# Fused attention and two MLP stages on one core: scales of v spread by ones-products instead of through DRAM, weights of norm loaded contiguously, first maxima of v taken later

## The chip, the cores and the metric

One core of one Trainium2 chip runs the whole program. The metric is the device time of one execution in microseconds (us), lower is better; the runs of a kernel are summed up by their median.

## What is computed

```python
# q, k, v: 4 batches x 12 heads x 448 x 64; x: 4 x 448 x 768
s = einsum('bhij,hg->bgij', 0.125 * q @ k.T, w_pre)          # heads mixed before softmax
p = softmax(s)
a = einsum('bhij,hg->bgij', p, w_post) @ v                   # heads mixed after it
x = a as (batch, 448, 768)
u, v = split(gelu_tanh(x @ w_in)); v_n = norm(v) * g_ln      # 768 -> 2 x 512
x = x + (u * (w_sg @ v_n + b_sg)) @ w_out
t = x @ w_theta; y = w_tok_r @ (x * cos t) + w_tok_i @ (x * sin t)
u = x + y; out = u + max(u @ w_ch, 0)
```

## The kernel before, in words

The program is one long list of instructions that Python writes out in order; every engine takes its own in that order. `attention` walks over 180 **blocks**: a block is 10 rows of the score matrix with all 12 heads (120 partitions x 448). A **tile** is up to 120 rows (12 blocks, or 9 for the rest), four tiles make a batch. The loop over `s` writes for each step several stages of different blocks, so that they overlap:

- `relayout(s+7)`: SP issues the DMA `blk<-s` (L217), which puts rows of the scores into the block's layout; five buffers.
- `premix(s+4)`: two products `psB` (L223) on TensorE; `rowmax(s+4)` `nmx` (L229) on DVE.
- `expo(s+3)` `e` (L236) on ACT; then `recip` on POOL (L244), `recip2` on DVE (L250), `p_hi` on POOL (L255), `p_lo` `pl` on DVE (L262).
- `postmix(s)`: twelve products `psC` (L277 to L280); `at_hi` (L302, ACT) and `at_lo` `al` (L308, DVE) for block s-1.
- `scores`: products `psA` of the tile after next (L203), copied out by ACT (L207, L209).

Between them three tables are called at fixed steps: `early` (mostly DMA issues, written behind `relayout`), `work` (products, behind `p_lo`) and `late` (at the end of the step). `put(table, s, fn)` enters a call. `attn_v` multiplies with v (L329), `turn_x` transposes the result into the PSUM tile `psT` (L342), which ACT empties (L349, L352).

v goes into the products as two fp16 halves, scaled by a power of two for each of its 768 channels. `load_vT` (L133) brings v transposed, channels on partitions, two pieces of 128 channels at a time; there are two buffers, so the third load of a batch waits for the first `v_max` (L148, DVE), which takes the maxima. `v_scale` (L87 to L95, L156) makes the scales `sv`, 128 partitions x 6. `v_mul` (L178, POOL) needs them along the free axis of every partition, as `vbc`, 128 x 768. So `v_scale_out` (L162) writes `sv` to DRAM with an access pattern of 4-byte elements, and `v_scale_in` (L166) reads the 3 KB back into all partitions. SP issues both; the second waits until the first has landed.

`put_v(b, s, m, gap)` enters this: `v_scale` at s, out at s+2, in at s+5, and from step m on `load_v`, `v_mul`, `v_hi`, `v_lo` piece by piece. For batch 0 the loads of vT stand at steps -7 to -5, the maxima at -6 to -4, s is -3 and m is 5; the loop starts at step -7. For batches 1 to 3 s is 7 steps ahead of the batch's first block and m 2 to 4 steps behind it.

Ahead of the loop stand the warm-up products (L421), the loads of q and k, the scores of the first tile, and `consts`. Decoding jobs of the later stages' float64 weights are woven in (`da`, `dp`, `dl`, `dh`; L588 to L631).

After attention the dense stages run as a list of units with calls ahead (`pre`) and behind (`post`) each. Where the first MLP starts, `rest` (L710, L712) loads `gln` (512 weights of norm, 128 x 4, each a 4-byte element in DRAM) and `bsg`; right behind them SP issues `wsgraw` (L727, L730), which ACT casts and DVE splits (`wsg`, L557, L560) for the `gate` products. `gln` is used in L834.

Of the kernel before, what the change touches and what calls it, by code (L numbers as in the profile page):

```python
# [6 lines left out]
F32 = mybir.dt.float32  # L7
F32R = mybir.dt.float32r
# [3 lines left out]
AF = mybir.ActivationFunctionType  # L12
# [4 lines left out]
B, H, S, D = 4, 12, 448, 64  # L17
NP = H // 2
DM = H * D
IB = 10  # L20
TI = IB * 12
TILES = [(t0, min(TI, S - t0)) for t0 in range(0, S, TI)]
LDS = (7, 4, 3, 2, 1, 4, 4, 5)
LD, LB, LE, LH, LL, EB, PB, SB = LDS
# [9 lines left out]
VM = 5  # L34
# [3 lines left out]
def attention(tc, nc, io, xT, B, extra, tail):  # L38
# [17 lines left out]
    with ExitStack() as es:  # L56
# [14 lines left out]
        cp = pool("a_const", 1)  # L71
# [8 lines left out]
        vsc_p = pool("a_vsc", 2)  # L80
        psB = pool("psB", 2, space=PSUM)
        psC = pool("psC", 2, space=PSUM)
        psD = pool("psD", 1, space=PSUM)
# [15 lines left out]
        wh = cp.tile([TI, H, IB], F16, name="wh")  # L99
        wl = cp.tile([TI, H, IB], F16, name="wl")  # L100
        dwp = cp.tile([128, NP], F32, name="dwp")
        ident = cp.tile([TI, TI], F32, name="ident")

        def consts():
            kpost = sm_p.tile([TI, H, IB], F32, tag="kpost", name="kpost", bufs=1)
            nc.sync.dma_start(out=kpost, in_=io["kpost"].rearrange("p (g i) -> p g i", g=H))
            nc.sync.dma_start(out=ident, in_=io["ident"][:TI, :TI])
            wrep = sm_p.tile([128, H, H], F32, tag="wrep", name="wrep", bufs=1)
            nc.sync.dma_start(out=wrep, in_=io["w_postT"].rearrange("g h -> (g h)").partition_broadcast(128)
                                .rearrange("p (g h) -> p g h", g=H))  # L110
            mx = sm_p.tile([128, H], F32, tag="wmx", name="wmx", bufs=1)
            nc.vector.tensor_reduce(out=mx, in_=wrep, axis=AX.X, op=ALU.max, apply_absolute_value=True)
            sw = sm_p.tile([128, H], F32, tag="sw", name="sw", bufs=1)
            dw = sm_p.tile([128, H], F32, tag="dw", name="dw", bufs=1)
            pow2(sw, dw, mx, H)
            nc.vector.tensor_tensor(out=kpost, in0=kpost,
                                    in1=sw[:TI].unsqueeze(2).to_broadcast([TI, H, IB]), op=ALU.mult)
            nc.vector.tensor_copy(wh, kpost)
            nc.vector.tensor_tensor(out=wl, in0=kpost, in1=wh, op=ALU.subtract)
            for e in range(2):  # L120
                nc.vector.tensor_scalar(out=dwp[64 * e:64 * e + 64], in0=dw[64 * e:64 * e + 64, e::2],
                                        scalar1=8.0, scalar2=None, op0=ALU.mult)


        raws, kt, qt = {}, {}, {}
# [12 lines left out]
            nc.sync.dma_start(out=qt[b, t][:, :NP * n], in_=io["qT"][b, :, NP * t0:NP * (t0 + n)])  # L138

        vt, dsc, vsb = {}, {}, {}  # L140
        vs_dram = es.enter_context(tc.tile_pool(name="a_vsd", bufs=1, space=bass.MemoryType.DRAM))
        vs_d = vs_dram.tile([B, DM], F32, name="vs_d")

        def v_max(b, c):
            if c == 0:
# [11 lines left out]
            dsc[b] = ds  # L157
            raws["sv", b] = sv

        def v_scale_out(b):  # L160
            with nc.allow_non_contiguous_dma(reason="768 scales"):
                nc.sync.dma_start(out=vs_d[b].rearrange("(c p) -> p c", p=128), in_=raws.pop(("sv", b)))  # L162

        def v_scale_in(b):
            bc = vsc_p.tile([128, DM], F32, tag="vbc", name="vbc", bufs=1)
            nc.sync.dma_start(out=bc, in_=vs_d[b].partition_broadcast(128))  # L166
            vsb[b] = bc

        def load_v(b, c):
            vt[b, c] = [v_p.tile([128, 4, 128], F16, tag=f"{t}{c}", name=t) for t in ("vh", "vl")]  # L170
# [190 lines left out]
        early, work, late = {}, {}, {}  # L361

        def put(d, s, fn, *a):
            d.setdefault(s, []).append((fn, a))
# [9 lines left out]

        def put_v(b, s, m, gap):
            put(late, s, v_scale, b)
            put(early, s + 2, v_scale_out, b)
            put(early, s + 5, v_scale_in, b)
            for c in range(NP):
                put(early, m - 2, load_v, b, c)  # L380
                put(late, m, v_mul, b, c)
                put(late, m + 2, v_hi, b, c)
                put(late, m + 3, v_lo, b, c)
                m += gap

        for T in range(2, nt):
            b, t = tiles[T]
# [3 lines left out]
            if t == 0:  # L391
                for c in range(NP):
                    put(early, unit(T - 1, c), load_k, b, c)
                for c in range(0, NP, 2):
                    s = unit(T - 1, c)
# [3 lines left out]
        for T in range(nt):  # L399
            b, t = tiles[T]  # L400
            l = last[tiles[T]]
            for c in range(NP):
                s = l + DD[t][c]
# [27 lines left out]
            scores(0, 0, c)  # L431
        consts()
        for c in range(0, NP, 2):
            put(early, -LD + c // 2, load_vT, 0, c)
            put(late, -LD + 1 + c // 2, v_max, 0, c)
        put_v(0, -LD + 4, VM, 2)
        for s in range(-LD, NB + 12):
            if s == -LD:
                for fn, a in early.get(s - 1, []):
# [36 lines left out]
KD, KF = DM // 128, HF // 128  # L476
# [187 lines left out]
def moe1(d, left, right):  # L664
# [37 lines left out]
    def rest():  # L702
        tail_ps.close()
        for name, bufs in (("w", 1), ("u", 1), ("vn", 1), ("t", 2), ("dec", 1)):
            d.open(name, bufs, left)
        d.open_psum(8, right)
        w = d.pools["w"]
        gln = w.tile([128, KF], F32, name="gln")
        with nc.allow_non_contiguous_dma(reason="512 values"):
            nc.sync.dma_start(out=gln, in_=io["g_ln"].rearrange("(k p) -> p k", p=128))  # L710
        bsg = w.tile([128, S], F32, name="bsg")
        nc.sync.dma_start(out=bsg, in_=io["b_sg"].partition_broadcast(128))  # L712
        small.update(gln=gln, bsg=bsg)
# [182 lines left out]
    for b in range(B):  # L896
# [8 lines left out]
        if b + 1 < B:  # L905
            i = u0[b] + KF
# [291 lines left out]
def layout(i):  # L1198
# [9 lines left out]
    for x in range(IB):  # L1208
# [11 lines left out]
        "kpost": kpost.reshape(TI, TI),  # L1220
        "w_postT": f(i["w_post"].T),
        "w_in": w64(i["moe_w_in"]),
        "g_ln": f(i["moe_g_ln"]),
        "w_sgT": f(i["moe_w_sg"].T),
        "b_sg": f(i["moe_b_sg"]),
        "w_out": w64(i["moe_w_out"]),
# [23 lines left out]
```

## Time and profile before

| what | value |
|---|---|
| median of 3 runs | 1045.97 us (1043.34 to 1046.72) |
| the profiled execution's own time | 1047.47 us |
| its span, first to last instruction | 1045.6 us |
| mean granted TensorE clock | 0.978 of full speed |
| PE / DVE / POOL / ACT busy, share of the span | 94% / 74% / 60% / 56% |

PE is TensorE's products, PEld its weight loads, SPq the issue of a DMA by SyncE. A busy share is an average over stages with different limits; what a stage is bound by is read from its own stretch. The attention blocks run from about 15 to 500 us, the first MLP to about 745 us, the rest is the second.

### The profile page before, as it was taken

The page shows a single profiled execution, that of the slowest core. Times are in us where ns is not written, and L with a number is a line of the kernel's source. Part 1 is how long each engine was busy: PE and PEld are TensorE (multiplying, and loading weights), DVE is VectorE, ACT ScalarE, POOL GpSimd, SP SyncE. Part 2 cuts the span into 40 slices and gives each one's busy share as a digit, 9 for nine tenths or more (in the row PEclk, how much of TensorE's full clock was granted, in tenths as well). Part 3 has the DMA queues.
Part 4 walks back from the last instruction along what each step waited for, and adds up shares of the span by engine and source line. Part 5 has one row for each costly group of instructions (what it writes and reads, how often), then busy time and mean ns, then how long its engine had stood idle before and what let it go on. Part 6 is the DMA issues. An engine that isn't in the chain of part 4 may idle for free.

```text
span 1045.6 us, 21830 instructions
## 1 busy us (share of the span) xinstructions
PE 982.3 (94%) x7848; PEld 742.7 (71%) x7848; DVE 775.5 (74%) x1458; ACT 586.6 (56%) x1374; POOL 622.4 (60%) x818
## 2 busy tenths in 40 slices
PE   7789999999999999997978999799999999999998
PEld 2445655565656555566756979587888999999997
DVE  2799878987888878985989998898896724925611
ACT  4577778786777778775754645454364412613310
POOL 0596558754686548854656877775666643753622
PEclk9899999999999999998989999999999999999999
DMA  5757565556556564347353676758956131130021
GB/s 191 154 167 221 142 139 183 180 168 129 161 193 203 131 158 152 131 108 265 113 155 89 213 225 199 229 188 274 335 184 226 41 106 31 32 106 16 31 76 53
DMA packets 135504, 159.47 MB, mean 153 GB/s; under 512 B 30309, under 2 KB 120933, under 8 KB 135397
## 3 DMA queue, kind: packets, MB, share of 16 engines
q1 hardware_dynamic: 135397, 158.08, 50.3%
q8 instruction: 63, 1.03, 0.4%
q14 instruction: 44, 0.36, 0.1%
HBM read 86.66 MB, written 32.85 MB: 114 GB/s over the span
## 4 chain that ended last, share of the span: by engine, by line
PE 57%; DVE 20%; DMA 9%; POOL 5%; issue 4%; ACT 3%; SPq 1%; DVEq 0%; ACTq 0%; POOLq 0%
PE ps L564 27%; PE psB L223 10%; PE psA L203 5%; PE psD L329 5%; DVE da L604 3%; PE psC L280 3%; PE psC L277 3%; DMA blk<-s 2%; PE psC L278 2%; DVE pl L262 2%; DVE da L602 2%; DVE dp L610 2%; DMA xres<-xT 2%; DVE dp L618 2%; DMA xraw<-xT 1%
## 5 line engine op out<-in xcount | busy, mean ns | idle before, releaser
L255 POOL TENSOR_SCALAR ph<-e,rc 120x448 f16<-120x448 f32 x180 | 163.9, 911 | 147.3 <-DVE rc L250 99.8
L223 PE MATMUL psB<-blk,kpre 120*120 120x448 f32 x360 | 177.3, 575 | 13.0 <-DMA blk<-s 8.2
L229 DVE TENSOR_REDUCE nmx<-psB 120x1 f32<-120x448 f32 x180 | 111.3, 618 | 49.9 <-PE psB L223 40.8
L262 DVE SCALAR_TENSOR_TENSOR pl<-e,rc,ph 120x448 f16<-120x448 f32 x180 | 147.4, 819 | 0.0
L236 ACT ACTIVATE e<-psB,nmx 120x448 f32<-120x448 f32 x180 | 114.3, 635 | 43.1 <-DVE nmx L229 43.0
L308 DVE SCALAR_TENSOR_TENSOR al<-psC,ah 128x480 f16<-128x480 f32 x180 | 116.1, 645 | 8.2 <-ACT ah L302 7.9
L277 PE MATMUL psC<-wh,ph 120*128 120x120 f16 x720 | 97.7, 218 | 10.9 <-DVE al L308 7.1
L302 ACT ACTIVATE ah<-psC 128x480 f16<-128x480 f32 x180 | 103.0, 572 | 7.6 <-PE psC L280 4.9
L209 ACT ACTIVATE s<-psA 120x896 f32<-120x896 f32 (+1 forms) x90 | 82.5, 917 | 42.5 <-PE psA L203 41.1
L564 PE MATMUL ps<-wtok,z 128*128 128x448 f32 x504 | 104.8, 368 | 0.4 <-POOL z L560 0.4
L564 PEld LDWEIGHTS ps<-wtok,z 128*128 128x128 f32 x504 | 94.4, 188 | 10.1 <-POOL z L560 0.8
L277 PEld LDWEIGHTS <-ph 120*128 120x128 f16 x720 | 68.8, 99 | 44.3 <-issue 18.6
L278 PE MATMUL psC<-wl,ph 120*128 120x120 f16 x720 | 97.1, 218 | 2.4 <-issue 2.4
L329 PEld LDWEIGHTS <-ah 128*128 128x128 f16 x1536 | 76.6, 99 | 31.2 <-issue 31.2
L203 PE MATMUL psA<-k,q 64*120 64x448 f32 (+1 forms) x384 | 96.2, 580 | 1.0 <-ACT s L209 1.0
L564 PE MATMUL ps<-wth,x2s 128*128 128x384 f32 x504 | 92.5, 338 | 2.0 <-POOL x2s L560 2.0
L564 PE MATMUL ps<-u,wch 128*128 128x448 f32 x432 | 89.9, 368 | 0.0
L564 PEld LDWEIGHTS ps<-wth,x2s 128*128 128x128 f32 x504 | 87.2, 188 | 2.8 <-POOL x2s L560 2.6
L560 POOL TENSOR_TENSOR z<-zz,z 128x384 fp32r<-128x384 f32 x56 | 61.9, 1125 | 45.8 <-ACT z L557 45.8
L564 PEld LDWEIGHTS ps<-u,wch 128*128 128x128 f32 x432 | 81.0, 188 | 8.1
L278 PEld LDWEIGHTS <-ph 120*128 120x128 f16 x720 | 71.2, 99 | 14.4 <-issue 14.2
L329 PE MATMUL psD<-vl,ah 128*128 128x64 f16 x768 | 78.0, 194 | 1.1 <-POOL vl L185 1.1
(124 smaller groups left out, 2171.9 us busy)
## 6 DMA issues: line engine op xcount, KB each, us to landing
blk<-s SPq DMA_DIRECT2D x176, 210.0 KB
draw<-in_w_in SPq DMA_DIRECT2D x24, 256.0 KB
vraw<-in_vN SPq DMA_DIRECT2D x24, 256.0 KB
k<-in_kvT SPq DMA_DIRECT2D x24, 224.0 KB
vT<-in_kvT SPq DMA_DIRECT2D x12, 448.0 KB
xraw<-xT SPq DMA_DIRECT2D x24, 224.0 KB
xres<-xT SPq DMA_DIRECT2D x24, 224.0 KB
x2T<-xres SPq DMA_DIRECT2D x24, 224.0 KB
```

The source lines that it names most:

```text
L203: nc.tensor.matmul(ps[e][:n, :S], q[p, o:o + n], k[p], start=True, stop=True)
L223: nc.tensor.matmul(ps[:r, :S], kpre[:r, :r], sblk.pop(s)[:r], start=True, stop=True)
L229: nc.vector.tensor_reduce(out=m[:r], in_=mix[s][:r, :S], axis=AX.X, op=ALU.max, negate=True)
L236: nc.scalar.activation(out=e[:r], in_=mix.pop(s)[:r, :S], func=AF.Exp, bias=nmx.pop(s)[:r], accum_out=sm[:r])
L255: nc.gpsimd.tensor_scalar(out=p[:r], in0=ex[s][0][:r], scalar1=rec[s][:r], scalar2=0.0, op0=ALU.mult, op1=ALU.add)
L262: nc.vector.scalar_tensor_tensor(out=p[:r], in0=ex.pop(s)[0][:r], scalar=rec.pop(s)[:r], in1=ph[s][:r], op0=ALU.mult, op1=ALU.subtract)
L277: nc.tensor.matmul(ps[:, jc, :, :n], cols(a, jc), wh[:r, :, :n], start=(jc == 0), stop=False)
L278: nc.tensor.matmul(ps[:, jc, :, :n], cols(a, jc), wl[:r, :, :n], start=False, stop=False)
L302: nc.scalar.activation(out=at_view(s, at[b, t][0]), in_=src, func=AF.Copy, scale=2.0 ** -17)
L308: nc.vector.scalar_tensor_tensor(out=al, in0=src, scalar=2.0 ** -17, in1=ah, op0=ALU.mult, op1=ALU.subtract)
L329: nc.tensor.matmul(ps[:, o:o + 64], a[:, i0:i0 + 128], v[:, jc, 64 * e:64 * e + 64], start=(o == 0 and m == 0), stop=(o == 320 and m == le ...
L564: self.nc.tensor.matmul(ps, l, r, start=(i == 0), stop=(i == len(terms) - 1))
```

## The change

The scales no longer go through DRAM. `v_diag` lets ACT write, for each of the six pieces, the identity times the piece's scales (a diagonal 128 x 128 matrix); `v_spread` multiplies a matrix of ones with three such diagonals at once (128 x 384), which puts each scale into all partitions of the PSUM tile `psT`, and ACT copies that to `vbc`. The identity grows from 120 x 120 to 128 x 128, and one more ACT operation makes the ones. In batches 1 to 3 (g = 1) the parts are spread over steps s+1 to s+6, in batch 0 over s+1 to s+3. `gln` comes as 128 contiguous runs of 16 bytes, its array being transposed on the host. For batch 0 the loads of vT move to steps -5 to -3, the maxima to -2 to 0, and `v_scale` from -3 to 1; m stays.

```diff
-        ident = cp.tile([TI, TI], F32, name="ident")
+        ident = cp.tile([128, 128], F32, name="ident")
+        ones = cp.tile([128, 128], F32R, name="ones")
...
-            nc.sync.dma_start(out=ident, in_=io["ident"][:TI, :TI])
+            nc.sync.dma_start(out=ident, in_=io["ident"])
+            nc.scalar.activation(out=ones, in_=ident, func=AF.Copy, scale=0.0, bias=1.0)
...
-        def v_scale_out(b):
-            with nc.allow_non_contiguous_dma(reason="768 scales"):
-                nc.sync.dma_start(out=vs_d[b].rearrange("(c p) -> p c", p=128), in_=raws.pop(("sv", b)))
-
-        def v_scale_in(b):
-            bc = vsc_p.tile([128, DM], F32, tag="vbc", name="vbc", bufs=1)
-            nc.sync.dma_start(out=bc, in_=vs_d[b].partition_broadcast(128))
-            vsb[b] = bc
+        def v_diag(b, c):
+            if c == 0:
+                raws["dg", b] = vsc_p.tile([128, NP, 128], F32R, tag="dg", name="dg", bufs=1)
+                vsb[b] = vsc_p.tile([128, DM], F32, tag="vbc", name="vbc", bufs=1)
+            nc.scalar.activation(out=raws["dg", b][:, c], in_=ident, func=AF.Copy, scale=raws["sv", b][:, c:c + 1])
+
+        def v_spread(b, half):
+
+            ps = psD.tile([128, 512], F32, tag="psT", name="psV", bufs=1)
+            nc.tensor.matmul(ps[:, :384], ones, raws["dg", b][:, 3 * half:3 * half + 3], start=True, stop=True)
+            nc.scalar.activation(out=vsb[b][:, 384 * half:384 * half + 384], in_=ps[:, :384], func=AF.Copy)
...
             put(late, s, v_scale, b)
-            put(early, s + 2, v_scale_out, b)
-            put(early, s + 5, v_scale_in, b)
+            g = 1 if b else 0
+            for c in range(NP):
+                put(late, s + 1 + g * (c // 2), v_diag, b, c)
+            for half in range(2):
+                put(work, s + 2 + half + g * (2 + half), v_spread, b, half)
...
-            put(early, -LD + c // 2, load_vT, 0, c)
-            put(late, -LD + 1 + c // 2, v_max, 0, c)
-        put_v(0, -LD + 4, VM, 2)
+            put(early, -LD + 2 + c // 2, load_vT, 0, c)
+            put(late, -2 + c // 2, v_max, 0, c)
+        put_v(0, 1, VM, 2)
...
-        with nc.allow_non_contiguous_dma(reason="512 values"):
-            nc.sync.dma_start(out=gln, in_=io["g_ln"].rearrange("(k p) -> p k", p=128))
+        nc.sync.dma_start(out=gln, in_=io["g_ln"])
...
-        "g_ln": f(i["moe_g_ln"]),
+        "g_ln": f(i["moe_g_ln"].reshape(KF, 128).T),
```

## Rows read from the trace of the kernel before

**Rows 1.** The page: busy time, share of the span and instructions of two engines.
```profile
PE   982.3 (94%) x7848; PEld 742.7 (71%) x7848; DVE 775.5 (74%) x1458; ACT 586.6 (56%) x1374; POOL 622.4 (60%) x818
```

**Rows 2.** The chain that ended last, 20 to 40 us: start, length, what.
```profile
20.91 3.46 DMA vT<-in_kvT
...
27.23 11.20 DMA blk<-s
```

**Rows 3.** SP's timeline, 14 to 37 us: start, length, line, what, how many.
```profile
14.58 0.94 SPq L217 DMA_DIRECT2D blk<-s  x1
...
26.74 0.38 SPq L162 DMA_DIRECT2D vs_d<-sv  x1
27.23 1.69 SPq L217 DMA_DIRECT2D blk<-s  x2
...
36.90 0.35 SPq L166 DMA_DIRECT2D vbc<-vs_d  x1
```

**Rows 4.** Stretches: PE, PEld, DVE, ACT, POOL busy, clock, DMA share, GB/s.
```profile
30.00:32.00 2.00, 2.00 (x16) 1.02 (x15) 1.79 (x5) 1.55 (x4) 1.54 (x5) 1.00 0.63 8
...
34.00:36.00 2.00, 0.00 (x0) 0.00 (x0) 0.49 (x1) 0.58 (x3) 1.11 (x2) 1.00 0.41 13
...
38.00:40.00 2.00, 1.43 (x2) 0.63 (x3) 0.00 (x0) 0.00 (x0) 0.00 (x0) 0.50 0.96 226
```

**Rows 5.** Timelines of PE and DVE: first premix; maxima of blocks 0 and 7.
```profile
17.88 0.98 PE L223 MATMUL psB<-blk,kpre 120*120 120x448 f32 x2 [1.10 <-DMA blk<-s]
...
22.94 0.61 DVE L229 TENSOR_REDUCE nmx<-psB 120x1 f32<-120x448 f32 x1
...
40.42 0.62 DVE L229 TENSOR_REDUCE nmx<-psB 120x1 f32<-120x448 f32 x1 [5.93 <-PE psB L223]
```

**Rows 6.** Groups by line, 18 to 41 us: DVE's operations, busy and mean ns.
```profile
L229 DVE TENSOR_REDUCE nmx<-psB 120x1 f32<-120x448 f32 x8 | 5.0, 620 | 6.2 <-PE psB L223 6.2
...
L148 DVE TENSOR_REDUCE vmx<-vT 128x2 f32<-128x896 f32 x3 | 3.3, 1087 | 9.1 <-DMA vT<-in_kvT 9.1
...
L262 DVE SCALAR_TENSOR_TENSOR pl<-e,rc,ph 120x448 f16<-120x448 f32 x4 | 2.7, 678 | 0.0
...
L308 DVE SCALAR_TENSOR_TENSOR al<-psC,ah 128x480 f16<-128x480 f32 x3 | 1.9, 650 | 0.0
...
L250 DVE RECIPROCAL rc<-rc 120x1 f32<-120x1 f32 x5 | 0.8, 158 | 0.3 <-POOL rc L244 0.2
```

**Rows 7.** Stretches behind the writes of batches 1, 2 and 3 (columns as in 4).
```profile
140.00:145.00 5.00, 4.04 (x47) 2.20 (x46) 2.83 (x6) 2.78 (x7) 2.23 (x4) 1.00 0.76 164
250.00:260.00 10.00, 7.82 (x72) 3.93 (x70) 5.03 (x13) 5.43 (x15) 3.36 (x6) 1.00 0.58 84
370.00:375.00 5.00, 3.02 (x27) 1.59 (x24) 1.43 (x4) 2.22 (x7) 0.95 (x2) 1.00 0.51 95
```

**Rows 8.** SP's timeline where the first MLP starts: loads behind gln.
```profile
520.29 0.43 SPq L710 DMA_DIRECT2D gln<-in_g_ln  x1
...
521.37 1.33 SPq L727 DMA_DIRECT2D wsgraw<-in_w_sgT  x3
```

**Rows 9.** Timelines of ACT and DVE there: the first cast and split of wsgraw.
```profile
527.79 0.58 ACT L557 ACTIVATE wsg<-wsgraw 128x448 fp32r<-128x448 f32 x1 [5.40 <-DMA wsgraw<-in_w_sgT]
...
528.40 0.62 DVE L560 TENSOR_TENSOR wsg<-wsgraw,wsg 128x448 fp32r<-128x448 f32 x1 [4.03 <-ACT wsg L557]
```

**Rows 10.** The stretch from that split to a wait for decoded wout (columns as in 4).
```profile
528.50:570.00 41.50, 32.19 (x122) 23.86 (x120) 40.70 (x62) 23.29 (x57) 29.41 (x29) 0.88 0.33 101
```

**Rows 11.** Timelines of ACT and PE: what the added work resembles.
```profile
150.78 0.86 ACT L349 ACTIVATE x<-psT,dsc 128x120 f32<-128x120 f32 x3
...
758.93 6.52 PE L564 MATMUL ps<-wth,x2s 128*128 128x384 f32 x36
```

**Rows 12.** Who waited for whom, whole span: TensorE's weight loads on ACT.
```profile
PEld psB L223 <- ACT e L236: 8.0, 7, 2.5
```

More of the change, by code (lines that the diff above doesn't have):

```diff
@@ L140, in attention @@
         vt, dsc, vsb = {}, {}, {}
-        vs_dram = es.enter_context(tc.tile_pool(name="a_vsd", bufs=1, space=bass.MemoryType.DRAM))
-        vs_d = vs_dram.tile([B, DM], F32, name="vs_d")
         def v_max(b, c):
```

## The prediction, as put on record before the run

> **What bounds the kernel now.** I read the page first: TensorE is busy for 94% of the span and no other engine for more than 74% [rows 1], so time is to be won where TensorE stands still, and each place has to be asked what it waits for. The chain of waits, read next, names a transfer in the start-up: a relayout of the scores that is issued at 27.23 us and takes 11.20 us [rows 2]. A relayout normally lands much faster: the first is issued at 14.58 and its premix starts at 17.88, after 3.3 us [rows 3, 5]. SP's timeline shows what stands ahead of the slow one: at 26.74 the 3 KB of scales go to DRAM, and SP can issue their read only at 36.90, when that write has landed, 10.2 us later [rows 3]. The stretches show the DMA engines meanwhile: busy for 0.63 and 0.41 of the time while 8 and 13 GB/s move; when the jam is over, 0.96 at 226 GB/s [rows 4]. So the engines work on many tiny pieces, and the relayouts issued behind them stand in line. TensorE does nothing from 34 to 36 us, and comes back at 0.50 of its clock, the level of 1.2 GHz [rows 4].
>
> The same write comes again ahead of batches 1, 2 and 3. There the relayouts are some blocks ahead, and most of the delay is hidden; what is left is TensorE's idle time in the stretch behind each write [rows 7]. The last place is the start of the first MLP, where gln, 512 pieces of 4 bytes, is issued just ahead of wsgraw [rows 8].
>
> **Start-up (term A).** Removed: the write, the read, and SP's wait between them. Moved: three loads of vT by two steps, past the relayouts of blocks 2 to 4 in SP's queue, and three maxima and the scales on DVE, from a time in which DVE waits to one in which it works. What limits the new start is DVE's own list up to the maximum of block 7, which now starts at 40.42 [rows 5]. The first premix ends at 17.88 + 0.98 = 18.9; today block 0's maximum starts only at 22.94, since the early maxima of v, which wait for their loads, stand ahead of it in DVE's queue [rows 5]. From 18.9 on DVE has to do, by mean durations [rows 6]: 8 maxima of blocks, 8 x 0.62 = 5.0; 4 pl, 4 x 0.68 = 2.7; 2 al, 1.3; 5 reciprocals, 0.8; 3 maxima of v, 3 x 1.09 = 3.3; the scales, six operations, which I price like the reciprocals, 1.0. That is 14.1 us, so 33.0; I add 0.5 for waits and take 33.5: a gain of 40.42 - 33.5 = 6.9.
>
> The ends of this term: at most the whole wait of 5.93 ahead of block 7's maximum and the whole 4.1 by which block 0's is late, 10.0 together [rows 5]. At the low end stands the third load of vT: with two buffers it waits for the first maximum, which now stands behind block 2's, and the relayouts of blocks 5, 6 and 7 wait behind it in SP's queue. By my list the first maximum of v is done at 22 to 23, so the load is issued then and is there at 23 + 3.5 = 26.5 [rows 2], about when DVE comes to it. If SP is held longer, DVE loses up to another such load, 3.5, and the gain is 3.4. I take nothing for the half clock after the hole: the list of DVE, not TensorE, sets the pace there. ACT writes six diagonals, each like one of the three small copies that take 0.86 together, 0.29, so 1.7 us, and empties two products, each of 384 columns like those three together, 0.86, so another 1.7 [rows 11]. Just ahead of the hole ACT is busy for 1.55 of 2 us [rows 4]; at 14.1 / 8 = 1.76 a block it has some 0.4 free in each, and each block's exponentials stand a step ahead of their use, which covers the rest; I charge 0.4. Should ACT have nothing free, it is up to 3.4. The making of the ones (one more 0.29) falls between the last copy of the first scores and the next ones, and the larger identity is a transfer that nobody waits for; both cost nothing as long as that holds, 0.3 if not. A is -6.5, between -10 and -3.
>
> **Batches 1 to 3 (term B).** Idle TensorE time behind the three writes: 5 - 4.04, 10 - 7.82 and 5 - 3.02, that is 0.96 + 2.18 + 1.98 = 5.1 us [rows 7]. Without the write these relayouts come in time and this goes. Added for TensorE: two products of 384 columns per batch; 36 of that shape take 6.52, so 0.18 each, six of them 1.1 us. TensorE is the bound there, so they are paid in full. ACT's 3.4 us per batch lie over six steps with two small operations at a time. The first product stands two steps behind the diagonals that it reads, the second three, so I see no wait; its PSUM tile is also turn_x's, which uses it one step earlier, and ACT empties it within that step. No row shows this wait; it is bounded by nothing below and above by 2.5 us for each, the longest of 7 waits of TensorE for ACT's exponentials (8.0 in all) [rows 12]. I take 0.4 in all, near the lower end because of those steps between. B is -5.1 + 1.1 + 0.4 = -3.6, between -5.1 and 0.
>
> **Weights of norm (term C).** The first wsgraw is issued at 521.37 and cast at 527.79, 6.4 us later, and DVE, which has nothing else, stands 4.03 us until it can split it [rows 8, 9]. From there to 570 DVE is busy for 40.70 of 41.50 us [rows 10] and sets when wout is decoded, for which TensorE then waits. So what DVE gets earlier the end gets earlier; the lower clock in that stretch costs nothing extra. Without the jam wsgraw should take 3.3 us as the first relayout did, and about 0.7 for bsg ahead of it: 4.0, a gain of 2.4. The new gln has 128 pieces in place of 512; no row shows 16-byte pieces, and by the scales' 768 pieces in 10.2 us [rows 3] they would cost 1.7 us at most, beside bsg's transfer in good part. C is -2.4, between -4.0 (the whole wait) and 0 (16-byte pieces hold up as much).
>
> **Sum.** -6.5 - 3.6 - 2.4 = -12.5. The profiled execution took 1047.47, 1.5 more than the median of 1045.97; against its own time the sum gives 1035.0, against the median **1033.5**, which I predict.
>
> The Trainium skill bears on the terms' common root. Its page "DMA: Bandwidth & Descriptors", section "Anatomy of one DMA — SWDGE (gpsimd) path", fits a transfer, on another queue's path, as 2.0 us plus its bytes at 436 GB/s; the 3 KB would then be there in 2.0 us, and nothing would be won by taking them away. The trace has 10.2 us for it [rows 3] and decides against that fit. The same page's section "Bandwidth" puts a small packet at some 10.5 ns, which as an estimate makes 768 of them 8.1 us beside the 2.0; by that figure the trace agrees.
>
> **The rivals.** (1) *The tiny pieces are innocent*: the late relayouts come from the loads of vT and of the jobs that stand ahead, and these remain. Then nothing is won and the six products cost 1.1: 1047. Against it speak the busy engines at 8 GB/s [rows 4], and that the wait sits behind such a write four times of four. By the skill's fit above this would be the case; the same rows weaken it. Chance 0.05.
> (2) *The third load of vT takes the write's place* in SP's queue and A is only -3: 1037. For it speaks that SP takes its list in order; against it, that the load is about ready when DVE comes. Chance 0.2.
> (3) *More comes back*: A near -10, B and C near -4 each, so -18: 1028. It needs a DVE that overlaps its operations better than my list. Chance 0.12.
> (4) *Slower: the eight products wait on ACT*. They stand ahead of postmix in TensorE's queue, and all following blocks wait with them. If each waits 2.5 us [rows 12], 20 us are lost against 6.9 + 5.1 + 2.4 = 14.4 won: 1051.5. It decides from 14.4 / 8 = 1.8 us a product. The steps between speak against it. Chance 0.05.
>
> **How the numbers follow.** The forecast, some 3 us to either side, has 0.58. The range takes in rivals 2 and 3 and most of the terms' ends, which will not all fall together: 1027 to 1041. Three of these cases are faster, 0.9; rival 1 lies within 0.3% (3 us, about what a measurement can tell here), 0.05; rival 4 is slower, 0.05.
>
> **What would show it.** The relayout of block 7 lands some 3 us after its issue, and block 7's maximum starts near 33.5; no stretch of the start shows busy DMA engines at 10 GB/s, and the clock does not fall to 0.50 there. The three later stretches show TensorE full, with products of 384 columns of 0.18 us and no wait ahead of them. wsg is cast about 4 us after its issue and DVE's 4.03 us shrink to 1.6. I am wrong if relayouts are still 10 us late without the write, if SP stands long at a load of vT, or if the new products wait for ACT.

## The result, and the profile after

The changed kernel takes 1034.9 us in the median of 4 runs (1032.56 to 1037.39) against 1045.9 of the kernel before beside it: ratio 0.9889, 95% interval 0.9856 to 0.9922. Predicted were 1033.5 us, a range of 1027 to 1041, and faster. In a later comparison the same pair gave 1034.97 (6 runs) and 1044.26 (17 runs), ratio 0.9905 (0.9882 to 0.9928). The profiled execution took 1037.39 us, its span is 1035.4 us, 10.2 less than before.

The page's first part, to be held against [rows 1]: only ACT has clearly more to do, 595.6 us against 586.6.

```profile
PE 982.6 (95%) x7856; PEld 744.0 (72%) x7856; DVE 773.5 (75%) x1458; ACT 595.6 (58%) x1407; POOL 622.9 (60%) x818
```

A busy share tells little of where 10 us went. The same events in both timelines tell more. I cut each execution at four of them: the start of the first scores (`psA`), the maximum of block 7 (`nmx`), the maximum of the last block, and the first gate product's scaling by `gln` (`gt`). **A** is from the first scores to block 7, **B** from there to the last block, **C** from there to the gate; the rest is the span less these. The table has every profiled execution of this study (us; the letter and number are those of the experiments below).

| execution | first scores | A | B | C | rest | span |
|---|---|---|---|---|---|---|
| before | 7.64 | 32.78 | 435.19 | 69.75 | 500.2 | 1045.6 |
| c1, before with `gln` contiguous | 6.37 | 32.94 | 430.95 | 70.99 | 499.1 | 1040.3 |
| after | 7.71 | 27.70 | 429.78 | 69.47 | 500.7 | 1035.4 |
| after, again | 7.60 | 26.85 | 430.15 | 69.99 | 500.3 | 1034.9 |
| e1 old maxima | 6.89 | 30.30 | 429.64 | 67.23 | 500.4 | 1034.5 |
| e2 third load late | 6.65 | 25.88 | 430.19 | 67.59 | 500.1 | 1030.4 |
| e3 `gln` behind | 7.57 | 26.71 | 430.19 | 69.51 | 502.1 | 1036.1 |
| e4 scattered write | 7.32 | 26.69 | 431.86 | 69.29 | 502.5 | 1037.7 |
| e5 write, 24-byte pieces | 7.63 | 27.71 | 429.61 | 69.50 | 498.0 | 1032.4 |
| e6 spread twice | 7.39 | 26.75 | 440.79 | 68.82 | 501.3 | 1045.0 |
| e7 `gln` strided | 7.07 | 26.96 | 429.93 | 67.62 | 502.9 | 1034.5 |
| e8 bias behind | 6.14 | 26.96 | 429.67 | 65.81 | 501.2 | 1029.8 |
| e9 bias behind, `gln` strided | 7.27 | 26.69 | 430.20 | 66.52 | 501.8 | 1032.5 |
| b1, e2 and e8 together | 6.37 | 25.87 | 430.09 | 66.08 | 499.5 | 1027.9 |

Two columns that no edit touches vary: the first scores by 1.6 us, the rest by 4.9. The experiments also ran on several chips: beside e1 to e4 the kernel before took 1042.09 us, beside e5 to e8 1045.2, one run each. So the time of one execution settles nothing below 2 to 3 us, while in the changed kernels A repeats to 1 us (e1, e2 and b1 aside, which edit it) and B to 0.6 (e4 and e6 aside, which edit it). Before against after, the 10.2 us of span are A 5.1, B 5.4 and C 0.3, less 0.5 in the rest and 0.1 at the first scores. The sum came out near the prediction; its terms did not: they were -6.5, -3.6 and -2.4.

**The start-up after.** SP's timeline, where the write and the read stood in [rows 3]:

```profile
19.25 0.81 SPq L220 DMA_DIRECT2D blk<-s  x1
24.30 0.38 SPq L135 DMA_DIRECT2D vT<-in_kvT  x1
24.78 3.58 SPq L220 DMA_DIRECT2D blk<-s  x4
```

SP now stands for some 4 us in front of the third load of vT, and four relayouts wait behind it. DVE's timeline shows what it waits for (the first `vmx`), and what follows (columns: start, length, then in brackets the idle time before it and what ended it):

```profile
18.70 0.62 DVE L232 TENSOR_REDUCE nmx<-psB 120x1 f32<-120x448 f32 x1 [6.37 <-PE psB L226]
20.58 0.62 DVE L232 TENSOR_REDUCE nmx<-psB 120x1 f32<-120x448 f32 x1 [1.26 <-PE psB L226]
22.47 0.62 DVE L232 TENSOR_REDUCE nmx<-psB 120x1 f32<-120x448 f32 x1 [1.26 <-PE psB L226]
...
23.21 1.07 DVE L148 TENSOR_REDUCE vmx<-vT 128x2 f32<-128x896 f32 x1
...
30.54 0.62 DVE L232 TENSOR_REDUCE nmx<-psB 120x1 f32<-120x448 f32 x1 [1.68 <-PE psB L226]
...
35.41 0.62 DVE L232 TENSOR_REDUCE nmx<-psB 120x1 f32<-120x448 f32 x1
```

Block 0's maximum starts 4.2 us earlier than in [rows 5] and block 7's 5.0 earlier. The wait of 5.93 us ahead of block 7's is gone; a wait of 1.68 ahead of block 5's is new. TensorE's timeline shows its cause, the premix of block 5, which waits for its relayout, and ahead of it one of the products of scores that stand between the first premixes. The chain of waits now has a transfer of 3.76 us, issued at 24.78, where [rows 2] has 11.20:

```profile
18.59 1.02 PE L206 MATMUL psA<-k,q 64*120 64x448 f32 x4
...
28.68 1.82 PE L226 MATMUL psB<-blk,kpre 120*120 120x448 f32 x2 [1.98 <-DMA blk<-s]
```

The stretches (columns as in [rows 4]) show a hole again, and the lower level of 1.2 GHz behind it, but no engines that are busy at 10 GB/s:

```profile
26.00:28.00 2.00, 0.70 (x13) 0.53 (x11) 2.00 (x5) 0.71 (x3) 1.01 (x3) 0.92 0.83 315
28.00:30.00 2.00, 1.32 (x2) 0.63 (x3) 0.85 (x1) 0.48 (x2) 0.66 (x4) 0.50 0.70 234
30.00:32.00 2.00, 2.00 (x14) 1.62 (x13) 1.46 (x4) 0.72 (x3) 0.11 (x1) 0.50 0.77 258
...
34.00:36.00 2.00, 2.00 (x20) 1.45 (x19) 1.94 (x5) 2.00 (x8) 0.98 (x2) 0.87 0.77 204
```

The fall of the clock is not in every execution. In the second one of the changed kernel TensorE waits for the same relayout, the clock stays at 1.00, the premix takes 0.98 us and DVE's wait ahead of block 5's maximum is 0.96. There TensorE stands a little later, ahead of the first product of the spread, for ACT's diagonals:

```profile
28.70 0.98 PE L226 MATMUL psB<-blk,kpre 120*120 120x448 f32 x2 [2.10 <-DMA blk<-s]
...
33.58 0.44 PE L169 MATMUL psV<-dg,ones 128*128 128x384 f32 x1 [0.77 <-ACT dg L164]
```

**Batches 1 to 3 after.** The same places as in [rows 7], shifted by what was gained ahead of them: TensorE is full in all three.

```profile
135.00:140.00 5.00, 5.00 (x53) 2.50 (x52) 4.22 (x10) 3.97 (x11) 2.23 (x4) 1.00 0.71 234
244.00:254.00 10.00, 10.00 (x114) 6.10 (x113) 7.87 (x18) 9.44 (x26) 6.14 (x10) 1.00 0.21 71
359.60:364.60 5.00, 5.00 (x62) 3.20 (x60) 3.81 (x11) 5.00 (x16) 1.31 (x3) 1.00 0.19 56
```

The new tile, `psV`, in the view of one tile: eight products, and in this execution hardly a wait ahead of the work on it. A record of 0.69 us begins while a premix product of 0.54 us is still running, 0.03 us behind its start, and ends 0.18 us behind its end.

```profile
L169 PE MATMUL psV<-dg,ones x8: 457/688/689, 34.9 to 367.2; 128*128 128x384 f32 x8
...
its engine sat idle before it (us, times) until:
  PE psV L169: 1.2, 3
  issue: 1.0, 5
  ACT x L352: 0.6, 2
```

**The first MLP after.** SP's timeline and those of ACT and DVE, which answer to [rows 8, 9]:

```profile
510.31 0.42 SPq L715 DMA_DIRECT2D gln<-in_g_ln  x1
510.79 1.66 SPq L717 DMA_DIRECT2D bsg<-in_b_sg  x1
512.55 1.33 SPq L732 DMA_DIRECT2D wsgraw<-in_w_sgT  x3
...
516.79 0.58 ACT L563 ACTIVATE wsg<-wsgraw 128x448 fp32r<-128x448 f32 x1 [4.38 <-DMA wsgraw<-in_w_sgT]
...
517.40 0.63 DVE L566 TENSOR_TENSOR wsg<-wsgraw,wsg 128x448 fp32r<-128x448 f32 x1 [3.02 <-ACT wsg L563]
```

`wsgraw` is cast 4.2 us after its issue, as predicted (4.0), but that issue comes 2.2 us behind `gln`'s instead of 1.1, because `bsg` now takes SP 1.66 us. DVE's wait shrinks by 1.0 us, not by 2.4.

### The profile page after: what moved, and what is told of

It reads as the page before. It is cut to its first block, busy times and chain, and to the rows that moved or that the text cites. A ratio compares the mean times of both kernels' runs of the same rounds, so it can differ in the third digit from the quotient of the medians.

```text
span 1035.4 us, 21866 instructions
## 1 busy us (share of the span) xinstructions
PE 982.6 (95%) x7856; PEld 744.0 (72%) x7856; DVE 773.5 (75%) x1458; ACT 595.6 (58%) x1407; POOL 622.9 (60%) x818
## 4 chain that ended last, share of the span: by engine, by line
PE 64%; DVE 17%; POOL 6%; ACT 5%; DMA 4%; issue 3%; SPq 1%; ACTq 0%; POOLq 0%; DVEq 0%
PE ps L570 34%; PE psB L226 10%; PE psA L206 6%; PE psD L332 5%; PE psC L283 3%; PE psC L280 3%; DVE pl L265 2%; DVE da L610 2%; PE psC L281 2%; DVE da L608 2%; DMA xraw<-xT 1%; DVE al L311 1%; POOL vraw L181 1%; POOL ph L258 1%; DVE dp L616 1%
```

## Experiments

All are edits of the changed kernel, but for c1. All compute the same outputs; e4 and e5 write 3 KB more per batch, which nobody reads, and e6 does work twice.

### The start-up: e1 and e2

e1 takes the move of the first maxima back:

```diff
-            put(early, -LD + 2 + c // 2, load_vT, 0, c)
-            put(late, -2 + c // 2, v_max, 0, c)
-        put_v(0, 1, VM, 2)
+            put(early, -LD + c // 2, load_vT, 0, c)
+            put(late, -LD + 1 + c // 2, v_max, 0, c)
+        put_v(0, -LD + 4, VM, 2)
```

> The changed kernel, with batch 0's loads of vT and maxima put back to where they were (steps -7 to -5 and -6 to -4, scales at -3, spread two and three steps behind). It measures the moved maxima alone. Theory (the third load of vT, behind its wait for the first maximum, holds the relayouts of blocks 5 to 8 in SP's queue, as the changed trace shows: issue at 24.78, landing 3.8 us later): without the move this wait comes earlier and blocks 5 to 8 are issued at about 21 to 25, so block 7's maximum, 35.41 in the changed kernel, starts at 34 to 35, and the span is 0 to 1.5 us shorter than 1035.4. Rival (the move is worth what block 0's maximum gained, 22.94 to 18.70): block 7's maximum comes at 38 to 39.5, and the span is 3 to 4 us longer.

A is 30.30: 2.5 us are won by the spread alone, and the move adds 2.6 to 3.6 (A is 26.7 to 27.7 in the nine executions with the changed order). DVE stands for vT three times ahead of its first blocks, as in the kernel before:

```profile
19.09 1.09 DVE L148 TENSOR_REDUCE vmx<-vT 128x2 f32<-128x896 f32 x1 [6.57 <-DMA vT<-in_kvT]
21.39 1.09 DVE L148 TENSOR_REDUCE vmx<-vT 128x2 f32<-128x896 f32 x1 [1.21 <-DMA vT<-in_kvT]
22.40 0.61 DVE L232 TENSOR_REDUCE nmx<-psB 120x1 f32<-120x448 f32 x1
```

The theory, by which the kernel is 0 to 1.5 us shorter without the move, is refuted; the 3 to 4 us of the rival are nearly it. The whole time of this run, 1036.5 us, doesn't show it, because C was 2.2 us shorter and the first scores came 0.8 us earlier than in the first execution of the changed kernel.

e2 keeps the move and issues the third load so late that SP needn't wait long for it:

```diff
-            put(early, -LD + 2 + c // 2, load_vT, 0, c)
-            put(late, -2 + c // 2, v_max, 0, c)
+            put(early, (-5, -4, -1)[c // 2], load_vT, 0, c)
+            put(late, (-2, -1, 1)[c // 2], v_max, 0, c)
```

> The changed kernel, with only batch 0's third load of vT moved on by two steps (-3 to -1), behind the relayouts of blocks 5 and 6 in SP's queue, and its maximum by one (0 to 1). Theory (SP's wait at that load is what blocks 5 and 6 lack): premix of block 5 no longer waits 1.98 us for its relayout, the clock stays at 1.00, and block 7's maximum starts at 33.4 to 34.2 in place of 35.41; the span is 1.2 to 2 us shorter than 1035.4. Rival (DVE's own list, with the maxima and scales, is the bound): block 7's maximum stays within 0.5 of 35.41, and so does the span.

A is 25.88, 0.8 to 1.8 us less. Block 5's premix no longer waits, and its maximum starts at 26.70 instead of 30.54 (1.1 us of this is the earlier start of the scores). A good part is lost again ahead of block 6: DVE has the last maximum of v and the scales in one piece. TensorE then stands 1.65 us for the diagonals, which ACT makes from these scales; this comes behind block 7's premix, so A doesn't hold it. The clock, expected to stay at 1.00, falls behind that hole, to 0.60 and 0.55 from 32 to 36 us.

```profile
26.70 0.62 DVE L232 TENSOR_REDUCE nmx<-psB 120x1 f32<-120x448 f32 x1
...
28.68 1.08 DVE L148 TENSOR_REDUCE vmx<-vT 128x2 f32<-128x896 f32 x1
...
30.78 0.61 DVE L232 TENSOR_REDUCE nmx<-psB 120x1 f32<-120x448 f32 x1
...
32.53 0.61 DVE L232 TENSOR_REDUCE nmx<-psB 120x1 f32<-120x448 f32 x1
```

TensorE's line:

```profile
31.66 0.45 PE L169 MATMUL psV<-dg,ones 128*128 128x384 f32 x1 [1.65 <-ACT dg L164]
```

So the load in SP's queue is a cause, but not worth the 3.5 us that I had put on it as the bound.

### The tiny pieces: e4 and e5

e4 brings back the write of the scales alone, in the batches 1 to 3. Nothing reads it and SP doesn't wait for its landing:

```diff
+        def v_scale_out(b):
+            with nc.allow_non_contiguous_dma(reason="768 scales"):
+                nc.sync.dma_start(out=vs_d[b].rearrange("(c p) -> p c", p=128), in_=raws["sv", b])
...
+            if b:
+                put(early, s + 2, v_scale_out, b)
```

> The changed kernel, and the scales of batches 1 to 3 written to DRAM in 4-byte pieces as before, though nothing reads them: SP never waits for that write. Theory (the pieces fill the DMA engines and what is issued behind them stands in line): the relayouts behind each write land about 10 us after their issue, TensorE stands still 1 to 2.5 us behind each, and the span is 4.5 to 6 us longer than 1035.4. Rival (it was SP's wait for the write's landing that made the blocks late): the span stays within 1 us of 1035.4.

e5 differs from it in one thing, the layout in DRAM: `"(p c) -> p c"`, 128 pieces of 24 bytes.

> The changed kernel, with the same extra write of the 768 scales after their computation in batches 1, 2 and 3 as in the run with the scattered write, and as there read by nobody, but in 128 pieces of 24 bytes (each partition's six scales side by side) instead of 768 pieces of 4. It tells the number of pieces from the write as such. Theory (the many tiny pieces jam the queue): 128 pieces land early and nothing behind them is late, so the three stretches stand within 0.4 us of the changed kernel in all, where the scattered write cost 2.5 us. Rival (any write there costs this, by its place in the queue of the sync engine and its long way): again 2 to 3 us in the three stretches.

With 768 pieces the stalls are back in all three places, between what theory and rival expected: 0.7, 1.1 and 0.7 us; B is 431.86, 1.7 to 2.1 us more than in the two executions of the changed kernel (0.7 us are regained between the first two places, as in e5, e6 and e8 too). With 128 pieces B is 429.61: nothing, as the theory had it. The middle stretch, e4 and then e5 (columns as in [rows 4]):

```profile
242.80:252.80 10.00, 9.02 (x113) 5.66 (x110) 7.35 (x17) 8.87 (x24) 5.12 (x9) 1.00 0.57 83
```

```profile
244.00:254.00 10.00, 10.00 (x109) 5.70 (x108) 7.89 (x18) 9.33 (x25) 6.54 (x10) 1.00 0.20 67
```

The DMA engines are busy 0.57 of the time for 83 GB/s with the scattered write, 0.20 for 67 without it. So it is the cutting into pieces, not a write as such; number and size of the pieces change together here. Whether a load from DRAM in as many pieces would do the same was not tried.

**Where the engines' time goes.** The prediction read the busy engines of [rows 4] as work "on many tiny pieces". The packets of the kernel before show something else. The write is issued at 26.74; first the stretch from 27 to 29 us, then the one from 29 to 36:

```profile
DMA packets 869, 0.14 MB, mean 69 GB/s; under 512 B 794, under 2 KB 869, under 8 KB 869
q1 hardware_dynamic: 869, 0.14, 37.0%
```

```profile
DMA packets 146, 0.25 MB, mean 35 GB/s; under 512 B 10, under 2 KB 136, under 8 KB 146
q1 hardware_dynamic: 146, 0.25, 69.1%
```

The last figure is the share of the 16 engines' time. The 768 pieces are among the 794 small packets of the first stretch, so by the records they are through after 2 us. In the seven us behind them there are 10 small packets, and the engines are busy for 69.1%: 0.53 us a packet, nearly all of them the rows of 1792 bytes that a relayout moves. In the start of the changed kernel, from 20 to 24 us, 650 packets take 80.7%, 0.08 us each. So the time is spent on the relayouts behind the write, as the prediction says of their lateness, but not on the pieces. e4 has the same from 242 to 247 us: 142 packets at 71.7%, 0.40 us each. What slows these rows no run shows.

It doesn't follow that the rest of B's 5.4 us is SP's wait for the landing; c1, below, shows why.

### The price of the spread: e6

```diff
-                put(late, s + 1 + g * (c // 2), v_diag, b, c)
+                for _ in range(1 + g):
+                    put(late, s + 1 + g * (c // 2), v_diag, b, c)
...
-                put(work, s + 2 + half + g * (2 + half), v_spread, b, half)
+                for j in range(1 + g):
+                    put(work, s + 2 + half + g * (2 + half) + j, v_spread, b, half)
```

> The changed kernel with the spread of batches 1 to 3 done twice (each diagonal made twice in its place, each product and copy repeated one block later; the result is the same). It prices the work that the change added. Theory (only TensorE's time counts, the diagonals and copies of ScalarE are hidden): six more products at 0.18 us and a little waiting, 0.2 to 0.5 us in each of three stretches, 0.6 to 1.5 us in all. Rival (ScalarE's nine or so more instructions and the products' waits for them are on the path): 12 us of ScalarE's work more in all, of which a third or more shows: 4 us or more.

The rival was right, and by more than it said: B is 440.79, 10.6 to 11.0 us more, for work of 3.4 us a batch on ACT (six diagonals at 0.40, two copies at 0.49) and two products on TensorE. ACT is full, and TensorE stands idle for it; the two stretches behind the diagonals of batch 1 and, from the view of `psV`, what the products waited for:

```profile
130.00:134.00 4.00, 3.17 (x46) 2.10 (x42) 2.14 (x5) 3.94 (x12) 2.85 (x5) 1.00 0.00 0
134.00:138.00 4.00, 3.03 (x18) 1.59 (x20) 1.79 (x5) 3.94 (x12) 1.06 (x3) 0.79 0.63 218
```

```profile
  ACT x L352: 7.0, 6
  ACT dg L164: 2.3, 2
```

The second line is batch 0's, which e6 leaves as it is; the first is that of batches 1 to 3. `x` is turn_x's result in `psT`: the product needs that tile, and ACT empties it only behind the diagonals that now stand in its queue. In the changed kernel ACT is at 3.97 of 5 us in the first of the three stretches, 9.44 of 10 in the second and 5.00 of 5 in the last, with TensorE still full. So the change uses ACT's free time nearly whole in the last two: what it adds is hidden, and not much more would have been.

### The weights of norm: e3, e7 and c1

e3 issues `gln` behind the five loads of `wsgraw`; e7 puts its strided form back in the changed kernel; c1 makes it contiguous in the kernel before (the change's part C alone).

```diff
-        nc.sync.dma_start(out=gln, in_=io["g_ln"])
...
+            nc.sync.dma_start(out=small["gln"], in_=io["g_ln"])
```

> The changed kernel, with the load of gln issued behind the five loads of wsgraw in place of ahead of bsg. Theory (128 pieces of 16 bytes still hold up what is behind them: in the changed trace bsg's issue takes 1.66 us in place of 0.50 and wsg is cast 6.5 us after gln's issue): bsg's issue takes 0.5 again, wsg is cast 1 to 2 us earlier against its step, DVE's wait of 3.0 us shrinks to 1 to 2, and the span is 1 to 2 us shorter. Rival (bsg's issue is held by the traffic of the w_out loads ahead of it): bsg's issue stays above 1.2 us and the span within 0.4 of 1035.4.

```diff
-        nc.sync.dma_start(out=gln, in_=io["g_ln"])
+            nc.sync.dma_start(out=gln, in_=io["g_ln"].rearrange("(k p) -> p k", p=128))
```

> The changed kernel with the normalization's weights loaded in 512 pieces of 4 bytes as before, so that all but this of the change is left. Theory (the strided load holds back the first weight matrices of the gate): their landing takes 6.4 us from issue as before and VectorE waits about 4.0 us for them, so 1 to 2 us are lost against the changed kernel between the end of the attention and the first normalization. Rival (the landing varies by what else is under way, whatever the shape of this load, as the run with the load moved behind suggests): VectorE's wait lies anywhere between 2 and 4 us and the time within 1 us of the changed kernel.

```diff
-            nc.sync.dma_start(out=gln, in_=io["g_ln"].rearrange("(k p) -> p k", p=128))
+        nc.sync.dma_start(out=gln, in_=io["g_ln"])
```

> The kernel before with one part of the change alone: the normalization's weights loaded contiguously. The forecast's term for it: VectorE's wait for the first cast weight of the gate shrinks from 4.03 to 1.6 us and the time falls by 2.4 us (ratio 0.998). Rival (the strided load of 512 pieces is not what delays the gate's weights, as the run without it in the changed kernel says): the wait lies between 2 and 4 us and the time is within 1.2 us of the kernel before (ratio 0.999 to 1.001).

C and DVE's wait for the first `wsg`: e3 69.51 and 3.94; e7 67.62 and 2.12; c1 70.99 and 4.51. The strided load gave the shortest of the three, and without any load of `gln` ahead of it `wsgraw` was as late as before, cast 6.9 us after its issue. For e7 the rival holds. For c1 neither does: DVE waits longer than the rival's 2 to 4 us, not less. In e3 `bsg`'s issue takes 0.42 us, as the theory has it, but the landing that was hoped for doesn't follow, and a reason isn't seen. The lines of DVE's timelines, of e3, e7 and c1 in this order:

```profile
517.25 1.21 DVE L566 TENSOR_TENSOR wsg<-wsgraw,wsg 128x448 fp32r<-128x448 f32 x2 [3.94 <-ACT wsg L563]
```

```profile
514.82 1.24 DVE L566 TENSOR_TENSOR wsg<-wsgraw,wsg 128x448 fp32r<-128x448 f32 x2 [2.12 <-ACT wsg L563]
```

```profile
524.43 1.33 DVE L560 TENSOR_TENSOR wsg<-wsgraw,wsg 128x448 fp32r<-128x448 f32 x2 [4.51 <-ACT wsg L557]
```

c1's median is 1042.11 (10 runs) against 1044.26, ratio 0.9984 (0.9968 to 1.0). That is the size predicted for this part, but in its profiled execution nothing of it stands at this place: C is 1.2 us longer than before, and the gain is in B, where c1 runs the same instructions as the kernel before. Whether c1's median is really lower stays open.

The packets of the kernel before could have told it. From 521 to 523 us, behind the issue of `gln` at 520.29, there are 545 small ones; the four us behind them:

```profile
DMA packets 624, 1.01 MB, mean 252 GB/s; under 512 B 74, under 2 KB 601, under 8 KB 623
```

The engines are busy for 93.2% there, 0.10 us a packet, and move 252 GB/s: nothing like the stretch behind the write of the scales.

c1 shows something else. Its B is 430.95, 4.2 us below that of the kernel before with all three writes in place. SP's timelines differ in one thing: the read of the scales is issued 9.67, 9.08 and 9.55 us behind the write in c1, 10.29, 10.08 and 10.57 in the kernel before. The pairs of batch 2, before and then c1:

```profile
246.70 0.39 SPq L162 DMA_DIRECT2D vs_d<-sv  x1
...
256.78 0.34 SPq L166 DMA_DIRECT2D vbc<-vs_d  x1
```

```profile
244.65 0.39 SPq L162 DMA_DIRECT2D vs_d<-sv  x1
...
253.73 0.34 SPq L166 DMA_DIRECT2D vbc<-vs_d  x1
```

So with 0.6 to 1.0 us less from write to read go 0.6, 1.6 and 1.7 us less of stall in the three batches. That the relayouts are ahead by about the length of the write, and that what is beyond is paid, would fit this; it is argued from three pairs of two executions, and no run tests it. B is worth 5.0 to 5.4 us against the one execution and 0.8 to 1.2 against the other.

### The bias: e8 and e9

In all these executions `bsg`, one row of 1.8 KB that goes to 128 partitions, stands ahead of `wsgraw`. e8 puts it behind; e9 does the same and makes `gln` strided again.

```diff
-        nc.sync.dma_start(out=bsg, in_=io["b_sg"].partition_broadcast(128))
...
+            nc.sync.dma_start(out=small["bsg"], in_=io["b_sg"].partition_broadcast(128))
```

> The changed kernel with the load of the gate's bias (one row of 1.8 KB spread over 128 partitions) issued behind the five loads of the gate's weights instead of ahead of them; the normalization's weights stay first. Theory (the bias, not the normalization's weights, now delays the gate's weights: its issue took 1.66 us in the changed kernel, and the engines of the queue run at a low rate just behind it): the weights land within 3.5 us of their issue, VectorE's wait falls below 2 us from 3.02, and the first normalization comes 1 to 2 us earlier. Rival (the order of these loads is without effect, the rate of all transfers there sets the landing): the wait stays at 2 to 4 us and the time within 0.5 us.

> The changed kernel with the gate's bias behind the gate's weights and the normalization's weights strided again (512 pieces of 4 bytes) in front of them. If the pieces of 4 bytes delay what is issued behind them, as the scattered scales of v did, the gate's weights must be late again: VectorE's wait goes from 0.71 us back to 2.5 us or more, and 2 us are lost against the run with the bias alone moved. Rival (the bias was the delay, the small pieces cost nothing here): the wait stays under 1.5 us and the first normalization within 0.8 us of that run, counted from the end of the attention.

C is 65.81 and 66.52, DVE's wait 0.71 and 1.17 us. First e8, then e9:

```profile
511.86 1.19 DVE L566 TENSOR_TENSOR wsg<-wsgraw,wsg 128x448 fp32r<-128x448 f32 x2 [0.71 <-ACT wsg L563]
```

```profile
513.88 1.25 DVE L566 TENSOR_TENSOR wsg<-wsgraw,wsg 128x448 fp32r<-128x448 f32 x2 [1.17 <-ACT wsg L563]
```

With b1, three executions have the bias behind: C is 65.8 to 66.5 there, and 67.2 to 71.0 in the eleven others. The theory of e8 held, and by more than it said (C is 3.7 to 4.2 us below the changed kernel's two); only the weights' landing, 3.7 us from issue to cast, was 0.2 later. Against the shortest of the eleven (e1, e2 and e7, 67.2 to 67.6) it is 1.4 to 1.8, so the size of the gain is less sure than its sign. Of e9 the rival held: the 512 pieces cost 0.7 us at most here. In all fourteen executions the gate's first scaling comes 16.7 to 17.3 us behind the split of the first weight, so C is decided ahead of that split, as the prediction has it.

### Both together: b1, and the changed kernel again

> The changed kernel with two further moves, each of which has been seen alone: the third load of v's transpose issued at block -1 and its maximum at block 1, and the gate's bias loaded behind the gate's weights. Theory (the two are independent: the first is worth 0.8 to 1.8 us at block 7 counted from the first scores, the second 2 to 3 us at the first normalization): 3 to 4.5 us under the changed kernel's median on the same chip, so about 1031. Rival (the gains seen in single executions were mostly the varying start of the first scores and the varying landing of the gate's weights): within 2 us of it.

> The changed kernel as it stands, for a comparison on the same chip. Theory (what was measured is what the change does): a ratio of 0.987 to 0.991 to the kernel before. In its trace, VectorE's wait for the first cast weight of the gate shows how much this varies between two executions of the same kernel: near 3.0 us again if the order of the loads sets it, anywhere from 2 to 4 us if it varies from execution to execution.

b1 is e2 and e8 in one kernel. Its median is 1030.88 us (5 runs, 1029.7 to 1033.92), ratio to before 0.9872 (0.985 to 0.9893); the changed kernel on the same chip 1034.97, ratio 0.9905 (0.9882 to 0.9928). The difference of 4.1 us is as expected, though the two intervals just overlap; less the 0.8 to 1.8 of e2 it leaves 2.3 to 3.3 us for the bias, an estimate. The traces place it: A 25.87 against 26.85 and C 66.08 against 69.99, 4.9 us together; what is left of the 7.0 us between these two spans lies in the columns that no edit touches. DVE's wait for `wsg` in the second execution of the changed kernel is 3.43 us, beside 3.02 in the first.

## Why the prediction was right, and where its terms were not

**The sum held, in part by luck.** Own time 1035.0 predicted, 1037.39 measured; median 1033.5 and 1034.9. Between the two profiled executions A gave 1.4 us less than forecast and C 2.1 less; B gave 1.8 more, and that belongs to the one execution of the kernel before. By the medians of the later comparison the gain is 9.3 us; with A's 5.1 to 6.2 and nothing for C, 3 to 4 are left for B, an estimate.

**A: right in mechanism, 0.3 to 1.4 us too large.** Predicted -6.5, measured -5.1 to -6.2. The failed step is "I add 0.5 for waits": DVE waits 1.26, 1.26 and 1.68 us ahead of blocks 1, 2 and 5, 4.2 in all, where my list ran on. The first two are TensorE's: it does the scores of a later tile between two premixes, so blocks come every 1.9 us. The third is the load of vT: I had it issued "at 22 to 23" and it went out at 24.30. That block 7 was late by 1.9 us and not by 3.7 is due to other errors of the list: its 14.1 us hold block 7's own maximum, 0.6, though they are counted to its start, and in the timeline one operation often starts before the end of the one ahead of it (a reciprocal at 24.90 of 0.15, `pl` at 24.97), so the other 13.5 us of durations take some 12.5. "I take nothing for the half clock" failed too, in the first execution: block 5's premix takes 1.82 us at it instead of 1.01, and DVE is waiting for just that, so 0.8 of the 1.68 are the clock's; in the second, at full clock, the wait is 0.96. ACT's 0.4 was about right: from block 7's maximum to block 8's it takes 3.04 and 3.18 us, before 2.80. By my cut this stands in B.

**Rival 2 was half of what happened.** Its mechanism is there, SP stands for the third load; its price was too high. e2, which removes the stand, wins 0.8 to 1.8, not 3.5.

**B: right in sign and place, its size the luck of an execution.** Predicted -3.6, measured -5.4 between the two profiled executions. The idle TensorE time of 5.1 went, and the products' 1.1 and ACT's 0.4 that I charged don't show: TensorE is full in the three stretches, and B fell by more than the 5.1. But the stall is not the same in two executions: 5.0 to 5.4 us of B in one, 0.8 to 1.2 in c1's. I read one profile as if the stall were fixed.

**C: wrong.** Predicted -2.4; the two executions have 69.47 and 69.99 against 69.75, so nothing. The failed step is "Without the jam wsgraw should take 3.3 us": there was no jam from `gln`. With 512 pieces e7 is not slower and e9 0.7 us at most, e3 is not faster with none ahead, and the packets behind `gln` run at 252 GB/s in the kernel before. What stood in front was `bsg`, which I had down for 0.7 us; moved behind, C falls by some 4 us against the changed kernel's two executions, by 2.3 to 3.3 as the medians have it.

**Rivals 1 and 4.** Tiny pieces are not innocent (e4 against e5), yet not each set of them is guilty (e7, e9): the guilty one is written to DRAM, the other read from it. "So the engines work on many tiny pieces" was misread; they work on the rows behind these, at 0.53 us each. The products' wait on ACT didn't come in batches 1 to 3. In batch 0 it was 0.77 us in the second execution and 1.65 in e2. And e6 shows how near it was: the second set of six products, with its diagonals and copies, costs 11 us, 1.8 each, which was the point from which that rival decides.

The Trainium skill's page "DMA: Bandwidth & Descriptors", section "Bandwidth", with some 10.5 ns a packet, gives as an estimate 8.1 us for the 768 pieces and 1.3 for 128; the 9.1 to 10.6 us from write to read and e5 without a stall agree with that in size. The packets don't: the 768 are recorded within 2 us, so the agreement that the prediction found is one of two numbers and not of a mechanism. By the same figure 512 pieces of `gln` are 5.4 us, and there it misleads too: 545 small packets are through in 2 us, and e9 loses 0.7 us at most to e8.

## What to carry to other kernels

A delay that ends behind a few us of cover is not a fixed price: read it from two executions before taking it as a gain: here the same three stalls cost 5.0 to 5.4 us in one and 0.8 to 1.2 in another. Busy DMA engines at a low rate don't say which packets they are busy with: count the packets by size in the stretch. When a small load is suspected of holding up the next one, move it away before reshaping it; the neighbour in the queue may be the one. And added work on an engine with room is free only up to that room: count it per step in the stretch where it falls, for the next piece of the same size can cost its whole length and more.

## What the runs showed of the hardware that was not expected

- A load of one 1.8 KB row into 128 partitions ahead of 0.9 MB of weights is followed by a late first weight: from the issue of the first of these loads to the cast of the first weight it takes 5.4 to 8.0 us in the eleven executions with the bias ahead, 4.1 to 4.6 in the three with it behind.
- A scattered write of 3 KB took 9.1 to 10.6 us in different executions of the same instructions, from its issue to that of the read that waits for it, though its 768 packets are recorded within 2 us; the rows of the relayout behind it took 0.53 us a packet instead of 0.08. The time from the start of a program to its first product of scores varied from 6.1 to 7.7 us.
- SP's issue of the same load at the same place took 1.66 us after and 0.42 in e1 and e2, where the three loads behind it took 2.41 and 2.85 us instead of 1.33. So SP was held somewhere among these issues by 1.1 to 1.5 us. In e8 and b1, with the bias behind, it is the first load of `wsgraw` that takes 1.38 and 1.39, so the hold isn't the bias's own; what holds SP stays open.
